# Weights decoded in the tile that they are read into, most reciprocals of two batches taken by way of DRAM, and new ranks, in a pooled-attention kernel with two feed-forward layers

## The chip, the cores and the metric

The kernel runs on one core of one Trainium2 chip. The metric is the device time in microseconds of one execution. The core has TensorE (PE in the rows, its weight loads PEld), VectorE (DVE), ScalarE (ACT), GpSimd (POOL) and SyncE (SP), which here issues most DMAs. TensorE has two levels of clock, 1.2 and 2.4 GHz; the profile gives the granted share.

## The reference

Four batches of eight heads; q, k and v have 1152 rows of 64. Pairs of rows of q are averaged, so 576 queries stand against 1152 keys; softmax with 1e-9 added to the sum; then two feed-forward layers over the 2304 rows of 512.

```python
q_pool = q.reshape(B, H, S // 2, 2, D).mean(axis=3)
scores = 1 / sqrt(D) * q_pool @ k.T
attn = exp(scores - max(scores))
x = attn / (attn.sum(-1) + 1e-9) @ v       # to (4 * 576, 512)
y = (s * relu(x @ w_in) ** 2 + b) @ w_out  # 512 -> 2048 -> 512
out = (sigmoid(y @ w_gate) * (y @ w_val)) @ w_out2   # 512 -> 1536 -> 512
```

The five weights come in as 64-bit floats. The kernel reads each as pairs of 32-bit words.

## The kernel before

Every large operand is split into a rounded high part and the rest, both in a format that TensorE multiplies at its full rate, and each product is made of three matmuls (lines 523 to 525 and 1000 to 1002) or, in the attention, of two or three.

*Attention.* The heads go in pairs. The first batch is done by rows of queries (`pair_rows`); the other three by columns (`pair_half`): each pair in two halves of 288 queries, each half for its two heads in turn. For one head `scores` makes nine blocks of 128 keys by 288 queries (line 752), ACT copies each to SBUF and DVE keeps a running maximum in a tile `mx`; the maximum goes over partitions by transposes (765, 730), is subtracted (DVE) and the exponent taken (ACT, 778). `half_head_sums` rounds the result to a high and a low part (`pp` tiles) and multiplies by v beside columns of ones (800, 801, 805), so that 64 rows of the bank hold x and the other 64 hold the same sum of the softmax, 64 times. ACT writes the sums of both heads, plus 1e-9, to one tile of 128x288 (810), DVE takes its reciprocal (822), and DVE or POOL multiplies x by it (823). In the second and third batch (`DIRECT`) x lies in a tile of SBUF that the feed-forward then splits (`load_split`); in the fourth, each half is stored to DRAM.

*Decode.* `decode` turns one 128x512 block of weights into high and low parts: a load of the pairs of words (`raw`, two tiles), a clamp of the upper words ("w top", 481, DVE or POOL, into a tile `dg`), a scaling ("w scale", ACT), a shift of the lower words ("w low", 485, DVE, into a tile `du`), two operations that join them ("w join" 488, "w sign" 491, DVE), a rounding ("w hi", ACT or POOL) and the rest ("w lo", DVE or POOL). There is one `dg` and one `du`. The first layer's 32 blocks are decoded for the first batch and kept in DRAM; later batches fetch them by POOL's queue (505). The second layer's 36 blocks are decoded twice, once for two batches each.

*Order.* Nothing is issued directly. All operations are added to a `Plan` with an engine or two, an assumed duration, the tiles they need from a number of rooms (`ROOM`) and a rank; `Plan.order` plays the whole program through with these durations and writes out one fixed order for each engine, SP's DMAs included. An engine takes the ready operation of the lowest rank. `MOVED` shifts the rank and the place in a tie of every kind of operation by a table written out by hand. On the chip each engine then works through its list strictly in order and waits by semaphores. So the feed-forward of one batch fills gaps of the attention of the next, as the table lets it.

Of the kernel before, what the change touches and what calls it, by code (L numbers as in the profile page):

```python
# [11 lines left out]
F32 = mybir.dt.float32  # L12
F32R = mybir.dt.float32r
AF = mybir.ActivationFunctionType
# [8 lines left out]


ROOM = dict(
    w=4, raw=2, dg=1, du=1, xy=2, xx=1, r=2, g=4,
    qn=1, kn=1, vn=1, qT=2, kT=2, vt=2, st=6, pp=6,
    sg=2, mx=3, mc=2, r3=2, ts=1, r9=2, x=1, o=2, s=2,
    yy=2, yl=1, h=4, fo=9,
    ps=4, pr=8, pm=1, acc=5, ff=6, p2=3, bank=8,  # L30
)
# [4 lines left out]


MOVED = {
    "q load": (-40, -122),
    "k load": (-5, -76),  # L40
    "v load": (44, 80),
    "v hi": (-12.5, -104),
    "v lo": (0, 12),
    "q add": (-28.5, 49),
    "q twice": (22, -83),
    "pr qT": (0, 83),
    "pr q hi False": (4.5, 33),
    "pr q lo False": (8, 30),
    "pr q hi True": (0, -76),
    "pr q lo True": (10, -85),  # L50
    "pr kT": (0, 17),
    "pr k hi": (-38.5, 40),
    "pr k lo": (-13, 67),
    "s b load": (0, -46),
    "r qk 1": (0, 238),
    "r max": (30, 219),
    "r - max": (-32, 31),
    "r exp": (21.5, -10),
    "r pT": (-18.5, -7),
    "r p": (-8, 9),  # L60
    "r p hi": (-2.5, -73),
    "r p lo": (-24.5, 146),
    "r pv": (-21, 58),
    "r pT hi": (-7, 104),
    "r pT lo": (44, 48),
    "r o": (-27.5, -23),
    "r x add": (52, -90),
    "r qk 2": (-1, -9),
    "r sums": (-8, -48),
    "r sums eps": (-24, -76),  # L70
    "r 1 / sums": (-9, -19),
    "r spread": (-22, -73),
    "r rows": (-1.5, -88),
    "r rows mid": (0, 341),
    "r x / sums": (0, -15),
    "r x / sums mid": (39, 38),
    "r end": (9.5, 29),
    "ps qT": (0, -24),
    "ps q hi False": (25.5, -60),
    "ps q lo False": (6, 36),  # L80
    "ps kT": (-0.5, -14),
    "ps k hi": (0, -132),
    "ps k lo": (-7, -33),
    "xx hi": (0, 74),
    "xx lo": (-12, -44),
    "w load": (-30, -37),
    "w top": (0, -2),
    "w scale": (-5.5, -17),
    "w low": (-13, -15),
    "w join": (-25.5, -49),  # L90
    "w sign": (-16, 89),
    "w hi": (-40, 12),
    "w lo": (-33.5, -64),
    "w keep": (-21, -47),
    "ff xx up": (46.5, -84),
    "ff relu": (0, 11),
    "square": (-30.5, -41),
    "g hi": (-1, -52),
    "g lo": (-32.5, -66),
    "ff down": (24, -66),  # L100
    "column sums": (58.5, -82),
    "column sum": (42, 14),
    "ff y": (-0.5, 39),
    "ff y add": (7.5, -20),
    "bias": (23, -78),
    "y bias": (19.5, -63),
    "y store": (-40, -99),
    "qk": (-3, -4),
    "s copy": (0, 41),
    "s max": (-0.5, 5),  # L110
    "max T": (0, -4),
    "max": (46.5, 5),
    "max rows": (13, -116),
    "s - max": (9.5, -46),
    "exp": (12.5, 16),
    "p hi": (-33.5, -85),
    "p lo": (51.5, -18),
    "pv hi": (13.5, -11),
    "pv lo": (20.5, 90),
    "sums": (14, 71),  # L120
    "x": (42.5, -28),
    "1 / sums": (60, 83),
    "x / sums": (11.5, -116),
    "w fetch": (42.5, -51),
    "w come": (-31, 87),
    "x store": (0, -158),
    "turn": (0, -29),
    "yy load": (-3, 83),
    "yy hi": (16, -21),
    "yy lo": (3, 111),  # L130
    "p2 yy up": (60, 26),
    "gate": (-30, 45),
    "gate val": (-5, 35),
    "h hi": (30, -36),
    "h lo": (28, 88),
    "down 2": (-36, 27),
    "out": (-11, 22),
    "out add": (5.5, 54),
    "out store": (-24, 145),
    "xx load": (59, -89),  # L140
    "p2 xx up": (-1.5, 27),
    "p2 relu": (0, 42),
    "p2 down": (0, -67),
    "p2 y": (-11.5, -107),
    "p2 y add": (0, 78),
}


# [193 lines left out]
def kernel(  # L342
# [124 lines left out]


    def decode(src, w, gate, rank):
        raw = slot("dec", "raw", [P, 512, 2], U32)  # L470
        g = slot("dec", "dg", [P, 512], F32)
        u = slot("dec", "du", [P, 512], U32)

        def fetch():
            if len(src.shape) == 3:
                nc.sync.dma_start(out=raw.t.rearrange("p (k f) t -> p k (f t)", f=P), in_=src)
            else:
                nc.sync.dma_start(out=raw.t.rearrange("p f t -> p (f t)"), in_=src)

        dma("w load", P * 4096, fetch, gate, [raw], rank)  # L480
        shared("w top", 512, lambda e: ENGINE[e].tensor_scalar(
            out=g.t, in0=raw.t[:, :, 1].bitcast(F32), scalar1=F64_TOP, scalar2=-F64_TOP, op0=ALU.min, op1=ALU.max,
        ), [raw], [g], rank, 3.66, fast=True)
        act("w scale", 512, lambda: nc.scalar.mul(g.t, g.t, 2.0 ** -112), [], [g], rank)
        dve("w low", 512, lambda: nc.vector.tensor_scalar(
            out=u.t, in0=raw.t[:, :, 0], scalar1=29, scalar2=None, op0=ALU.logical_shift_right,
        ), [raw], [u], rank, True)
        dve("w join", 512, lambda: nc.vector.scalar_tensor_tensor(
            out=u.t, in0=g.t.bitcast(U32), scalar=3, in1=u.t, op0=ALU.logical_shift_left, op1=ALU.bitwise_or,
        ), [g], [u], rank, port=True)  # L490
        dve("w sign", 512, lambda: nc.vector.scalar_tensor_tensor(  # L491
            out=u.t, in0=g.t.bitcast(U32), scalar=0x80000000, in1=u.t, op0=ALU.bitwise_and, op1=ALU.bitwise_or,
        ), [g], [u], rank, port=True)
        copy_sb("w hi", 512, lambda: w.t[:, 0, :], lambda: u.t.bitcast(F32), [u], [(w, 0)], rank)
        tt_sb("w lo", 512, lambda: w.t[:, 1, :], lambda: u.t.bitcast(F32), lambda: w.t[:, 0, :].bitcast(F32), ALU.subtract,
              [u, (w, 0)], [(w, 1)], rank)

    def weights(pair, gate=(), rank=FE, keep=False, kept=False):

# [290 lines left out]
    def half_head_sums(hf, j, qT, kT, vt, x, sums):  # L790
# [19 lines left out]
        act("sums", HQ + 112, lambda: nc.scalar.activation(  # L810
            out=sums.t[js], in_=acc.t[D:, :HQ], func=AF.Identity, bias=eps[D:, 0:1], scale=1.0), [acc], [(sums, j)], SK, sbuf=False)
        xt, xk = x
        copy_ps("x", HQ, lambda: xt()[js], lambda: acc.t[:D, :HQ], [acc], [(*xk, j)], SK)

    def pair_half(b, hp, hf, prep):
        qT, kT, vt = prep
        x = slot("sm", "x", [P, HQ]) if b not in DIRECT else xs[b]
        xt, xk = ((lambda: x.t[:, hp, hf * HQ:(hf + 1) * HQ]), (x, hp, hf)) if b in DIRECT else ((lambda: x.t), (x,))
        sums = slot("sm", "s", [P, HQ])
        for j in range(2):  # L820
            half_head_sums(hf, j, qT[j], kT[j], vt[j], (xt, xk), sums)
        dve("1 / sums", HQ * 6, lambda: nc.vector.reciprocal(out=sums.t, in_=sums.t), [], [(sums, 0), (sums, 1)], SK)
        tt_sb("x / sums", HQ, xt, xt, lambda: sums.t, ALU.mult,
              [(sums, 0), (sums, 1)], [(*xk, 0), (*xk, 1), *([(x, hp, hf)] if b in DIRECT else [])], SK)
# [6 lines left out]
    def pair_rows(hp, prep, x):  # L831
# [52 lines left out]
        def group(j, g, blocks, mid):  # L884
# [4 lines left out]
            for c0 in range(0, NK, step):  # L889
# [209 lines left out]
```

## Time and profile before

| | us |
|---|---|
| three runs | 1484.94, 1485.54, 1489.52 |
| median | 1485.54 |
| profiled execution | 1490.57 |
| its span, first to last instruction | 1488.8 |
| PE busy in the span | 1411.6 (95%) |
| DVE, ACT, POOL busy | 1111.9 (75%), 946.2 (64%), 667.6 (45%) |
| mean granted clock of TensorE | 0.981 |

The profiled execution is a fourth execution, with 5.0 us more than the median. Busy shares are over the whole span. The attention fills about the first 890 us; the last 600 are feed-forward alone.

### The profile page before, as it was taken

How to read it: one execution, taken by the hardware profiler on the slowest of the kernel's cores; microseconds unless marked ns; L12 is line 12 of the kernel's file. 1: busy time of each engine (PE TensorE's matmuls, PEld its weight loads, DVE VectorE, ACT ScalarE, POOL GpSimd, SP SyncE). 2: the span in 40 equal slices, each digit the busy share in tenths (PEclk: the TensorE clock that was granted, in tenths of full speed). 3: DMA queues.
4: the chain of work that ended last, by engine and by line, in shares of the span. 5: the costliest groups of instructions: out<-in, count | busy, mean ns of one | idle time of the engine just before them, and what ended most of it. 6: DMA issues, size and time to landing. Idle time of an engine off the chain costs nothing.

```text
span 1488.8 us, 26268 instructions
## 1 busy us (share of the span) xinstructions
PE 1411.6 (95%) x9868; PEld 1346.4 (90%) x9868; DVE 1111.9 (75%) x1848; ACT 946.2 (64%) x2030; POOL 667.6 (45%) x555
## 2 busy tenths in 40 slices
PE   7998899897979999999999999999999999999998
PEld 6887789897869999999999999989998999989897
DVE  6899898889998988888998867667674125757562
ACT  6889888868777989779889965434241524434140
POOL 3666465646575666547766635312222002313120
PEclk9999999899989999999999999999999999999999
DMA  3234313342532513323250335433234543333122
GB/s 88 77 117 155 105 57 106 122 145 94 179 112 82 177 35 144 125 68 103 74 190 24 130 141 204 163 99 99 72 100 121 184 170 100 100 96 103 58 71 64
DMA packets 98510, 165.79 MB, mean 111 GB/s; under 512 B 41936, under 2 KB 75728, under 8 KB 89296
## 3 DMA queue, kind: packets, MB, share of 16 engines
q1 hardware_dynamic: 91472, 113.79, 24.8%
q0 software_dynamic: 6912, 50.33, 9.5%
q8 instruction: 77, 1.26, 0.3%
q14 instruction: 49, 0.40, 0.1%
HBM read 137.89 MB, written 26.21 MB: 110 GB/s over the span
## 4 chain that ended last, share of the span: by engine, by line
PE 73%; DVE 11%; ACT 10%; issue 4%; POOL 1%; DMA 0%; DVEq 0%; ACTq 0%; POOLq 0%
PE banks L523 14%; PE banks L525 14%; PE banks L524 14%; PE banks L752 5%; PE banks L1000 3%; PE banks L1001 3%; PE banks L1002 3%; PE banks L800 3%; PE banks L801 3%; DVE mx L463 3%; PE banks L805 3%; PE banks L920 2%; ACT st L457 2%; PE banks L853 2%; ACT kT L457 2%
## 5 line engine op out<-in xcount | busy, mean ns | idle before, releaser
L525 PE MATMUL banks<-yy,w 128*128 128x288 f32 x768 | 226.4, 295 | 0.0
L524 PE MATMUL banks<-yy,w 128*128 128x288 f32 x768 | 226.2, 294 | 0.0
L523 PE MATMUL banks<-yy,w 128*128 128x288 f32 x768 | 226.0, 294 | 0.0
L460 POOL TENSOR_TENSOR pp<-st,pp 128x864 fp32r<-128x864 f32 x96 | 203.7, 2131 | 36.6 <-ACT pp L450 25.0
L457 ACT COPY st<-banks 128x288 f32<-128x288 f32 x432 | 154.0, 412 | 42.7 <-PE banks L752 31.0
L463 DVE TENSOR_TENSOR mx<-banks,mx 128x288 f32<-128x288 f32 x336 | 151.1, 451 | 27.3 <-ACT st L457 15.1
L752 PE MATMUL banks<-qT,kT 128*128 128x288 f32 x864 | 162.0, 308 | 6.0 <-DVE mx L463 3.8
L523 PE MATMUL banks<-xx,w 128*128 128x288 f32 x512 | 154.5, 302 | 1.6 <-ACT r L593 1.2
L524 PE MATMUL banks<-xx,w 128*128 128x288 f32 x512 | 151.1, 295 | 0.6 <-POOL xx L460 0.6
L525 PE MATMUL banks<-xx,w 128*128 128x288 f32 x512 | 151.0, 295 | 0.0
L463 DVE TENSOR_TENSOR st<-st,banks 128x864 f32<-128x864 f32 x144 | 146.5, 1042 | 5.0 <-PE banks L730 5.0
L778 ACT ACTIVATE st<-st 128x864 f32<-128x864 f32 x144 | 133.4, 936 | 24.2 <-DVE st L463 23.2
L450 ACT CAST w<-du 128x512 fp32r<-128x512 f32 x100 | 62.2, 622 | 132.6 <-DVE du L491 91.2
L523 PEld LDWEIGHTS banks<-yy,w 128*128 128x128 f32 x768 | 144.1, 188 | 0.3
L524 PEld LDWEIGHTS banks<-yy,w 128*128 128x128 f32 x768 | 144.0, 188 | 0.3
L525 PEld LDWEIGHTS banks<-yy,w 128*128 128x128 f32 x768 | 144.0, 188 | 0.0
L752 PEld LDWEIGHTS banks<-qT,kT 128*128 128x128 f32 x864 | 132.1, 195 | 11.3 <-DVE mx L463 6.6
L523 PE MATMUL banks<-g,w 128*128 128x288 f32 x448 | 138.6, 309 | 2.0 <-DVE mx L463 1.4
L800 PE MATMUL banks<-pp,vt 128*128 128x288 f32 x432 | 124.7, 308 | 10.6 <-ACT pp L450 7.5
L525 PE MATMUL banks<-g,w 128*128 128x288 f32 x448 | 133.1, 297 | 0.0
L524 PE MATMUL banks<-g,w 128*128 128x288 f32 x448 | 133.0, 297 | 0.0
L801 PE MATMUL banks<-pp,vt 128*64 128x288 f32 x432 | 121.4, 301 | 0.0
(147 smaller groups left out, 3895.6 us busy)
## 6 DMA issues: line engine op xcount, KB each, us to landing
w<-d_1u_1u POOLq DMA_DIRECT2D x24, 1024.0 KB, 6.1
w<-d_1d_1d POOLq DMA_DIRECT2D x24, 1024.0 KB, 6.2
raw<-in_moe_w_out_dram SPq DMA_DIRECT2D x40, 512.0 KB, 3.4
raw<-in_moe_w_gate_dram SPq DMA_DIRECT2D x24, 512.0 KB, 3.6
raw<-in_moe_w_val_dram SPq DMA_DIRECT2D x24, 512.0 KB, 3.5
qn<-in_q_dram SPq DMA_DIRECT2D x16, 576.0 KB, 4.5
kn<-in_k_dram SPq DMA_DIRECT2D x32, 288.0 KB, 4.1
vn<-in_v_dram SPq DMA_DIRECT2D x32, 288.0 KB, 2.8
```

Of the source, the lines that this page charges most:

```text
L450: nc.scalar.copy(out=out(), in_=in_())
L457: act(name, n, lambda: nc.scalar.copy(out=out(), in_=in_()), r, w, rank, sbuf=False)
L460: shared(name, n, lambda e: ENGINE[e].tensor_tensor(out=out(), in0=in0(), in1=in1(), op=op), r, w, rank, 2.15)
L463: dve(name, n, lambda: nc.vector.tensor_tensor(out=out(), in0=in0(), in1=in1(), op=op), r, w, rank)
L523: nc.tensor.matmul(ps(), lhsT=whi(), rhs=xhi(), start=first, stop=False)
L524: nc.tensor.matmul(ps(), lhsT=whi(), rhs=xlo(), start=False, stop=False)
L525: nc.tensor.matmul(ps(), lhsT=wlo(), rhs=xhi(), start=False, stop=last)
L752: nc.tensor.matmul(ps.t[:, :HQ], lhsT=kT.t[:, c], rhs=qq[:, w, hf * HQ:(hf + 1) * HQ], start=(w == 0), stop=(w == 1))
L778: act("exp", 3 * HQ, lambda s=s: nc.scalar.activation(out=s.t, in_=s.t, func=AF.Exp), [], parts, AT)
L800: nc.tensor.matmul(acc.t[:, :HQ], lhsT=vt.t[:, 3 * i + c, D:], rhs=hi.t[:, c], start=(i == c == 0), stop=False)
L801: nc.tensor.matmul(acc.t[:D, :HQ], lhsT=vt.t[:, 3 * i + c, :D], rhs=hi.t[:, c], start=False, stop=False)
L805: nc.tensor.matmul(acc.t[:, :HQ], lhsT=vt.t[:, 3 * i + c, D:], rhs=lo.t[:, c], start=False, stop=(i == c == 2))
```

## The change

Four groups of things are changed.

- `decode` keeps everything in `raw`: the upper words are clamped and scaled where they lie, the lower words shifted, joined and signed where they lie. Its operations thus read and write every second word. `dg` and `du` are gone; there are three `raw` tiles for two. The duration that the plan assumes for "w top" on POOL goes from 105 + 3.66 ns an element to 105 + 1.08.
- In the second and third batch, for all halves but each batch's last, the sums of the two heads (now written as one row each) go to DRAM as 2 x 288 numbers, come back as 64 rows of nine, are inverted there, go to DRAM again and come back spread over 64 rows for each head. The last half of each batch, and the whole fourth batch, keep the reciprocal of 128x288.
- Rooms: `mx` two tiles for three, `r9` one for two, new tiles `rs` and `rr`, one each; the first batch's output copy ("r o") takes a `pp` tile instead of one of its own.
- Each new operation has a rank of its own, and the table `MOVED` is written anew for all others too.

```diff
-    w=4, raw=2, dg=1, du=1, xy=2, xx=1, r=2, g=4,
+    w=4, raw=3, xy=2, xx=1, r=2, g=4,
...
-    sg=2, mx=3, mc=2, r3=2, ts=1, r9=2, x=1, o=2, s=2,
+    sg=2, mx=2, mc=2, r9=1, x=1, s=2, rs=1, rr=1,
...
-    "q load": (-40, -122),
+    "q load": (8, -97),
...
-    "w fetch": (42.5, -51),
-    "w come": (-31, 87),
+    "w fetch": (-8, 31),
+    "w come": (0, -52),
...
         raw = slot("dec", "raw", [P, 512, 2], U32)
-        g = slot("dec", "dg", [P, 512], F32)
-        u = slot("dec", "du", [P, 512], U32)
+        low, top = (raw, 0), (raw, 1)
+
+        def words(i):
+            return raw.t[:, :, i]
...
         shared("w top", 512, lambda e: ENGINE[e].tensor_scalar(
-            out=g.t, in0=raw.t[:, :, 1].bitcast(F32), scalar1=F64_TOP, scalar2=-F64_TOP, op0=ALU.min, op1=ALU.max,
-        ), [raw], [g], rank, 3.66, fast=True)
+            out=words(1).bitcast(F32), in0=words(1).bitcast(F32), scalar1=F64_TOP, scalar2=-F64_TOP, op0=ALU.min, op1=ALU.max,
+        ), [], [top], rank, 1.08, fast=True)
...
         dve("w low", 512, lambda: nc.vector.tensor_scalar(
-            out=u.t, in0=raw.t[:, :, 0], scalar1=29, scalar2=None, op0=ALU.logical_shift_right,
-        ), [raw], [u], rank, True)
+            out=words(0), in0=words(0), scalar1=29, scalar2=None, op0=ALU.logical_shift_right,
+        ), [], [low], rank, True)
         dve("w join", 512, lambda: nc.vector.scalar_tensor_tensor(
-            out=u.t, in0=g.t.bitcast(U32), scalar=3, in1=u.t, op0=ALU.logical_shift_left, op1=ALU.bitwise_or,
-        ), [g], [u], rank, port=True)
+            out=words(0), in0=words(1), scalar=3, in1=words(0), op0=ALU.logical_shift_left, op1=ALU.bitwise_or,
+        ), [top], [low], rank, port=True)
...
+    def inverse(sums, both):
+
+        uid[0] += 1
+        s_d, r_d = (dram.tile([2, HQ], F32, name=f"{n}_{uid[0]}") for n in ("s_d", "r_d"))
+        rs = slot("sm", "rs", [64, 2 * HQ // 64])
+        rr = slot("sm", "rr", [P, HQ])
...
+        dma("sums out", 2304, lambda: nc.sync.dma_start(out=s_d, in_=sums.t.rearrange("(j p) q -> j p q", j=2)[:, 0]),
+            both, [(rs, "out")], SK)
+        dma("sums in", 2304, lambda: nc.sync.dma_start(out=rs.t, in_=spread(s_d)), [(rs, "out")], [rs], SK)
+        dve("1 / sums spread", 54, lambda: nc.vector.reciprocal(out=rs.t, in_=rs.t), [], [rs], SK)
+        dma("1 / sums out", 2304, lambda: nc.sync.dma_start(out=spread(r_d), in_=rs.t), [rs], [(rr, "out")], SK)
+
+        def back():
+            for j in range(2):
+                nc.sync.dma_start(out=rr.t[j * D:(j + 1) * D], in_=r_d[j:j + 1, :].to_broadcast([D, HQ]))
+
+        dma("1 / sums in", P * HQ * 4, back, [(rr, "out")], [rr], SK)
+        return rr, [rr]
...
+        last = b == B - 1 or hp == NP - 1 and hf == 1
...
-        dve("1 / sums", HQ * 6, lambda: nc.vector.reciprocal(out=sums.t, in_=sums.t), [], [(sums, 0), (sums, 1)], SK)
+        if last:
+            dve("1 / sums", HQ * 6, lambda: nc.vector.reciprocal(out=sums.t, in_=sums.t), [], both, SK)
+            inv = sums
+        else:
+            inv, both = inverse(sums, both)
...
-            o = slot("sm", "o", [P, 320])
+            o = slot("pp", "pp", [P, 3 * HQ])
```

## Rows read from the trace of the kernel before

**Rows 1.** The page, busy tenths in 40 slices of 37.2 us, and clock.
```profile
PE   7998899897979999999999999999999999999998
...
PEclk9999999899989999999999999999999999999999
```

**Rows 2.** Stretches: start:end, length, busy us of engines (instructions), clock, DMA share, GB/s.
```profile
75.00:190.00 115.00, 99.14 (x668) 90.22 (x667) 102.67 (x216) 101.25 (x285) 66.27 (x71) 0.94 0.39 122
190.00:447.00 257.00, 225.08 (x1568) 215.48 (x1568) 230.20 (x357) 201.06 (x406) 155.38 (x111) 0.92 0.36 119
447.00:890.00 443.00, 432.15 (x3223) 417.37 (x3222) 384.60 (x617) 371.02 (x765) 269.17 (x199) 1.00 0.33 105
890.00:1489.00 599.00, 592.88 (x4009) 566.82 (x4008) 336.85 (x531) 215.66 (x406) 137.53 (x121) 1.00 0.35 114
```

**Rows 3.** PE's waits (total us, times, longest): two of 190:447, two of 447:890.
```profile
PE banks L800 <- ACT pp L450: 7.5, 1, 7.5
PE banks L765 <- DVE mx L463: 5.0, 2, 4.0
...
PE banks L730 <- DVE mc L769: 3.6, 6, 0.9
...
PE banks L765 <- DVE kT L463: 0.5, 2, 0.3
```

**Rows 4.** Tile s: duration ns min/median/max; and the 128x9 reciprocal (busy us, mean ns).
```profile
L810 ACT ACTIVATE s<-banks,eps x48: 496/498/502, 221.4 to 876.6; 64x288 f32<-64x288 f32 x48
L822 DVE RECIPROCAL s<-s x24: 1934/1942/1954, 227.3 to 877.1; 128x288 f32<-128x288 f32 x24
...
L943 DVE RECIPROCAL r<-r 128x9 f32<-128x9 f32 x4 | 0.8, 203 | 0.0
```

**Rows 5.** The reciprocals of line 822 alone, by stretch: DVE busy us (count).
```profile
190.00:452.00 262.00, 13.62 (x7) 0.92 0.37 121
...
495.00:700.00 205.00, 13.59 (x7) 1.00 0.36 116
700.00:890.00 190.00, 17.48 (x9) 1.00 0.31 103
```

**Rows 6.** Small DMAs: store of x (start ns, landing us), then loads of 512 bytes.
```profile
L827 SPq DMA_DIRECT2D x_d<-x x8: 319/326/332, 729.7 to 880.2; - x8
...
DMA to landing us min/median/max: 1.7/1.7/7.7
...
DMA to landing us min/median/max: 3.6/4.2/4.9
```

**Rows 7.** Decode steps over the span, ns min/median/max; the zeroing of qm (mean).
```profile
L481 POOL TENSOR_SCALAR dg<-raw x52: 635/654/1324, 70.9 to 1434.5; 128x512 f32<-128x512 f32 x52
L485 DVE TENSOR_SCALAR du<-raw x104: 362/427/2322, 74.1 to 1442.5; 128x512 uint32<-128x512 uint32 x104
L488 DVE SCALAR_TENSOR_TENSOR du<-dg,du x104: 673/692/3122, 75.1 to 1442.9; 128x512 uint32<-128x512 uint32 x104
...
L394 DVE CAST qm<-zero 128x512 fp32r<-128x512 f32 x1 | 0.4, 426 | 1.1 <-POOL eps L396 1.1
```

**Rows 8.** Waits of POOL and ACT in 190:447; the last over the span.
```profile
POOL dg L481 <- DVE du L491: 24.7, 8, 6.4
...
ACT w L450 <- DVE du L491: 10.1, 5, 3.3
...
POOL qn L460 <- DMA qn<-in_q_dram: 11.8, 4, 9.0
```

**Rows 9.** SP's own waits in 190:660, the first and the last of fifteen.
```profile
SPq L665 <- POOL vt L460: 98.7, 11, 19.8
...
SPq L478 <- DVE qT L709: 2.2, 2, 1.9
```

**Rows 10.** Join and low in 190:447: count, busy us, mean ns, idle before.
```profile
L488 DVE SCALAR_TENSOR_TENSOR du<-dg,du 128x512 uint32<-128x512 uint32 x23 | 25.2, 1098 | 0.1
L485 DVE TENSOR_SCALAR du<-raw 128x512 uint32<-128x512 uint32 x23 | 19.6, 850 | 0.9 <-POOL w L460 0.8
```

More of the change, by code (lines that the diff above doesn't have):

```diff
@@ L38 @@
 MOVED = {
-    "q load": (-40, -122),
[L40 to L123, printed above, removed]
-    "w fetch": (42.5, -51),
-    "w come": (-31, 87),
[L126 to L145, printed above, removed]
+    "q load": (8, -97),
+    "k load": (16, 21),
+    "v load": (58, -139),
+    "v hi": (-33.5, 17),
+    "v lo": (-5, -53),
+    "q add": (56.5, -16),
+    "q twice": (60, -3),
+    "pr qT": (0, -105),
@@ new lines @@
+    "pr q hi False": (1.5, -26),
+    "pr q lo False": (10, 70),
+    "pr q hi True": (40, 70),
+    "pr q lo True": (4, -76),
+    "pr kT": (-7, 0),
+    "pr k hi": (-23.5, 64),
+    "pr k lo": (4.5, 94),
+    "s b load": (51, 101),
+    "r qk 1": (0, 436),
+    "r max": (20, 94),
+    "r - max": (-33.5, 116),
+    "r exp": (59.5, -13),
+    "r pT": (-31, -29),
+    "r p": (-29.5, -47),
+    "r p hi": (-7.5, -76),
+    "r p lo": (-26.5, 53),
+    "r pv": (-40, 67),
+    "r pT hi": (-20, 30),
+    "r pT lo": (32.5, 157),
@@ new lines @@
+    "r o": (-40, 104),
+    "r x add": (27, -30),
+    "r qk 2": (-29, -108),
+    "r sums": (1.5, -33),
+    "r sums eps": (-0.5, -100),
+    "r 1 / sums": (30, -110),
+    "r spread": (-40, -92),
+    "r rows": (-3, 63),
+    "r rows mid": (0, 533),
+    "r x / sums": (0.5, 3),
+    "r x / sums mid": (52, 49),
+    "r end": (-1, -100),
+    "ps qT": (-6.5, -120),
+    "ps q hi False": (60, 55),
+    "ps q lo False": (-21, 2),
+    "ps kT": (-16, 90),
+    "ps k hi": (2, 116),
+    "ps k lo": (-33.5, 42),
@@ new lines @@
+    "xx hi": (8, 64),
+    "xx lo": (0, -25),
+    "w load": (-40, -77),
+    "w top": (-14.5, 44),
+    "w scale": (-24.5, -15),
+    "w low": (-21, -21),
+    "w join": (0, 65),
+    "w sign": (-30, -67),
+    "w hi": (-33, -111),
+    "w lo": (-40, 113),
+    "w keep": (-34.5, 128),
+    "ff xx up": (42.5, -17),
+    "ff relu": (0, -85),
+    "square": (0.5, 119),
+    "g hi": (0.5, 88),
+    "g lo": (-2, 74),
+    "ff down": (31, 10),
+    "column sums": (60, -1),
+    "column sum": (37.5, 56),
@@ new lines @@
+    "ff y": (-28.5, 61),
+    "ff y add": (19, 52),
+    "bias": (0, -21),
+    "y bias": (0, -25),
+    "y store": (0, -54),
+    "qk": (3.5, -109),
+    "s copy": (4, -73),
+    "s max": (7.5, 39),
+    "max T": (0.5, 25),
+    "max": (60, 105),
+    "max rows": (26.5, 9),
+    "s - max": (22, -81),
+    "exp": (0, 89),
+    "p hi": (-29.5, 0),
+    "p lo": (54.5, -68),
+    "pv hi": (22, 11),
+    "pv lo": (31, 60),
+    "sums": (26, -2),
+    "x": (38, -115),
+    "sums out": (-35, 44),
+    "sums in": (-9.5, 84),
@@ new lines @@
+    "1 / sums spread": (0, -60),
+    "1 / sums out": (-12, -13),
+    "1 / sums in": (22.5, -70),
+    "x / sums": (17, 25),
+    "1 / sums": (24.5, -96),
+    "w fetch": (-8, 31),
+    "w come": (0, -52),
+    "x store": (-3, -88),
+    "turn": (-9, -110),
+    "yy load": (16.5, -72),
+    "yy hi": (13.5, 59),
+    "yy lo": (0, -93),
+    "p2 yy up": (57.5, 61),
+    "gate": (-40, 69),
+    "gate val": (-25.5, 123),
+    "h hi": (0, -7),
+    "h lo": (59.5, 88),
+    "down 2": (-7, 35),
+    "out": (-23, -57),
@@ L146 @@
+    "out add": (11, -115),
+    "out store": (0, -50),
+    "xx load": (-40, 35),
+    "p2 xx up": (-1.5, 75),
+    "p2 relu": (0, -42),
+    "p2 down": (0, 97),
+    "p2 y": (0, -29),
+    "p2 y add": (8, 19),
 }
@@ L478, in fetch @@
                 nc.sync.dma_start(out=raw.t.rearrange("p f t -> p (f t)"), in_=src)
-        dma("w load", P * 4096, fetch, gate, [raw], rank)
+        dma("w load", P * 4096, fetch, gate, [low, top], rank)
         shared("w top", 512, lambda e: ENGINE[e].tensor_scalar(
-            out=g.t, in0=raw.t[:, :, 1].bitcast(F32), scalar1=F64_TOP, scalar2=-F64_TOP, op0=ALU.min, op1=ALU.max,
-        ), [raw], [g], rank, 3.66, fast=True)
-        act("w scale", 512, lambda: nc.scalar.mul(g.t, g.t, 2.0 ** -112), [], [g], rank)
+            out=words(1).bitcast(F32), in0=words(1).bitcast(F32), scalar1=F64_TOP, scalar2=-F64_TOP, op0=ALU.min, op1=ALU.max,
+        ), [], [top], rank, 1.08, fast=True)
@@ L485, in decode @@
+        act("w scale", 512, lambda: nc.scalar.mul(words(1).bitcast(F32), words(1).bitcast(F32), 2.0 ** -112), [], [top], rank)
         dve("w low", 512, lambda: nc.vector.tensor_scalar(
-            out=u.t, in0=raw.t[:, :, 0], scalar1=29, scalar2=None, op0=ALU.logical_shift_right,
-        ), [raw], [u], rank, True)
+            out=words(0), in0=words(0), scalar1=29, scalar2=None, op0=ALU.logical_shift_right,
+        ), [], [low], rank, True)
         dve("w join", 512, lambda: nc.vector.scalar_tensor_tensor(
-            out=u.t, in0=g.t.bitcast(U32), scalar=3, in1=u.t, op0=ALU.logical_shift_left, op1=ALU.bitwise_or,
-        ), [g], [u], rank, port=True)
+            out=words(0), in0=words(1), scalar=3, in1=words(0), op0=ALU.logical_shift_left, op1=ALU.bitwise_or,
+        ), [top], [low], rank, port=True)
@@ L491, in decode @@
         dve("w sign", 512, lambda: nc.vector.scalar_tensor_tensor(
[L492 to L496, printed above, removed]
+            out=words(0), in0=words(1), scalar=0x80000000, in1=words(0), op0=ALU.bitwise_and, op1=ALU.bitwise_or,
+        ), [top], [low], rank, port=True)
@@ L498, in weights @@
+        copy_sb("w hi", 512, lambda: w.t[:, 0, :], lambda: words(0).bitcast(F32), [low], [(w, 0)], rank)
+        tt_sb("w lo", 512, lambda: w.t[:, 1, :], lambda: words(0).bitcast(F32), lambda: w.t[:, 0, :].bitcast(F32), ALU.subtract,
+              [low, (w, 0)], [(w, 1)], rank)
     def weights(pair, gate=(), rank=FE, keep=False, kept=False):
@@ L788, in split_p, with half_head_sums @@
         return hi, lo
-    def half_head_sums(hf, j, qT, kT, vt, x, sums):
+    def half_head_sums(hf, j, qT, kT, vt, x, sums, rows):
         st = scores(hf, qT, kT)
@@ L810, in half_head_sums, with spread @@
         act("sums", HQ + 112, lambda: nc.scalar.activation(
-            out=sums.t[js], in_=acc.t[D:, :HQ], func=AF.Identity, bias=eps[D:, 0:1], scale=1.0), [acc], [(sums, j)], SK, sbuf=False)
+            out=sums.t[j * D:j * D + rows], in_=acc.t[D:D + rows, :HQ], func=AF.Identity, bias=eps[D:D + rows, 0:1], scale=1.0),
+            [acc], [(sums, j)], SK, sbuf=False)
         xt, xk = x
         copy_ps("x", HQ, lambda: xt()[js], lambda: acc.t[:D, :HQ], [acc], [(*xk, j)], SK)
+    def inverse(sums, both):
[3 more added lines that the diff above has]
+        rr = slot("sm", "rr", [P, HQ])
+        def spread(t):
+            return t.rearrange("j (p r) -> (j p) r", r=2 * HQ // 64)
+        dma("sums out", 2304, lambda: nc.sync.dma_start(out=s_d, in_=sums.t.rearrange("(j p) q -> j p q", j=2)[:, 0]),
[8 more added lines that the diff above has]
+        return rr, [rr]
     def pair_half(b, hp, hf, prep):
@@ L819, in pair_half @@
         sums = slot("sm", "s", [P, HQ])
+        last = b == B - 1 or hp == NP - 1 and hf == 1
         for j in range(2):
-            half_head_sums(hf, j, qT[j], kT[j], vt[j], (xt, xk), sums)
-        dve("1 / sums", HQ * 6, lambda: nc.vector.reciprocal(out=sums.t, in_=sums.t), [], [(sums, 0), (sums, 1)], SK)
-        tt_sb("x / sums", HQ, xt, xt, lambda: sums.t, ALU.mult,
-              [(sums, 0), (sums, 1)], [(*xk, 0), (*xk, 1), *([(x, hp, hf)] if b in DIRECT else [])], SK)
+            half_head_sums(hf, j, qT[j], kT[j], vt[j], (xt, xk), sums, D if last else 1)
+        both = [(sums, 0), (sums, 1)]
+        if last:
[3 more added lines that the diff above has]
+            inv, both = inverse(sums, both)
+        tt_sb("x / sums", HQ, xt, xt, lambda: inv.t, ALU.mult,
+              both, [(*xk, 0), (*xk, 1), *([(x, hp, hf)] if b in DIRECT else [])], SK)
         if b in DIRECT:
```

## The prediction

> **What bounds the kernel now.** I read the slices of the span first, then the busy times of the engines in five stretches cut where the slices change, then who keeps TensorE waiting in each stretch, and last the operations that the change touches.
>
> The slices show two kernels in one [rows 1]. From about slice 24 on PE shows 9 in every slice at full clock; before that it falls to 7 in places and the granted clock to 8. The stretches say it in numbers [rows 2]. In 890 to 1489 PE is busy 592.9 of 599 us: nothing that the other engines save there can be had. In 447 to 890 it is idle 443 - 432.2 = 10.8 us. In 190 to 447 it is idle 257 - 225.1 = 31.9 us and its clock is 0.92 on the mean, while DVE is busy 230.2 of 257 us (90%), ACT 78%, POOL 60%. So DVE is the nearest thing to a bound there, and the change's own operations lie there: the second batch's attention, the first batch's first feed-forward and the decode of its weights. In 75 to 190 DVE is at 89% and ACT at 88%, and PE is idle 15.9 us.
>
> The waits of PE agree: in 190 to 447 the largest single one ends on ACT, the next and most of the others on DVE, with the running maxima first [rows 3]. DVE is busy nine tenths of that stretch, so that it is late comes from its amount of work and from its order.
>
> **Reciprocals.** One of 128x288 takes 1.94 us; the 24 of them spread little, 1.934 to 1.954 [rows 4]. One of 128x9 takes 0.203 us [rows 4]; the new one has 64 rows of nine, and I take that price. Each replaced one gives DVE 1.943 - 0.203 = 1.74 us. Seven of eight are replaced in the second batch and seven of eight in the third, 14 x 1.74 = 24.4 us. By place [rows 5]: seven stand in 190 to 452 (second batch), the one in 452 to 495 is that batch's last and stays, the seven of 495 to 700 are the third batch's that go, and of the nine after 700 one is the third batch's last and eight the fourth's, which all stay.
>
> First seven: 7 x 1.74 = 12.2 us out of an engine that is busy 90% of the stretch. I count 0.9 of it, 11 us; the ends are 0 (the rest of the stretch is bound by the order) and 12.2 plus the 2.3 us that DVE waited for ACT's sums in front of two of them, 14.5. Second seven: again 12.2 us, but PE is idle 10.8 us in all of 447 to 890, and the waits that PE has there on DVE are six, from 3.6 down to 0.5 and 7.7 us together, the first and the last of them in [rows 3]. DVE loses 12.2 of 384.6 us of work, a thirtieth; I count 1 us, between 0 and 5.
>
> **The way by DRAM.** Per replaced reciprocal SP issues five DMAs: sums out, sums in, result out, and two broadcasts in. At 0.33 us a start [rows 6] that is 14 x 5 x 0.33 = 23 us of SP. The trip has four landings in a row. The nearest rows: the store of x, 144 KB, lands after 1.7 us at best, a load of 512 bytes to 128 rows after 3.6 and 4.9 [rows 6]. So a trip is 4 x 1.7 = 6.8 to 4 x 4.9 = 19.6 us, and I take 8. It ends in x / sums, whose target in these batches is the x tile that stays in SBUF; the next reader is the split at the batch's end, and the last half, the only one with no time to spare, keeps the old way. In 190 to 452 seven halves come, 37 us each. I count the trip at nothing: the following half hides it. If that cover is gone, one landing of 1.7 us per trip, 24 us over 14, is the price (the slower rival below). The sums instruction on ACT writes one row in place of 64, with the same 288 columns; I take its 0.498 us [rows 4] for the new one too, and if it fell to nothing ACT, at 78%, would gain 28 x 0.5 = 14 us beside the bound.
>
> **Decode in the tile.** All seven steps now walk over every second word; before, only the reads of top and low did. New to it are the writes of top and low, join and sign on DVE, scale on ACT, hi on ACT or POOL, lo on DVE or POOL. For one-input reads the trace shows the price: low reads every second word and takes 0.362 at best, 0.427 in the middle, where a 128x512 cast that walks no second words (the zeroing of qm) takes 0.426 [rows 7]. So reading is free there. No row shows such a write, or a two-input operation with such reads. Ends: nothing, or for 32 decodes up to 447 the loss of low's and top's rate (to join's 0.692, +0.27 each) and twice the time for join and its twin, sign (+0.69 each), 32 x (0.54 + 1.38) = 61 us of DVE. I take nothing, from the nearest row. The Trainium skill says in SBUF — State Buffer, section Door 1: The DMA port swizzle, that words in one 16-byte line come at full bandwidth with two or more hits per line; a step of 8 bytes has two. By that rule the sum would be the same and the strided rival falls away; the trace agrees for reads with the 0.427 us, and no row shows the writes.
>
> What the tile change removes is the two single buffers dg and du. POOL stands 24.7 us in 190 to 447 before w top, until the sign step of the decode before has let go of dg [rows 8], and w top is in order with POOL's lows of p, g and v. With three raw tiles that wait has no cause within three decodes. POOL is at 60% in that stretch and so no bound; ACT's casts lose 10.1 us to the same chain [rows 8]. I count 1 us, between 0 and 12. What is late next is the load: raw was free for its next load after low, and now only after lo. SP waits anyway, fifteen kinds of wait from 98.7 down to 2.2 us and 426 of the 470 us from 190 to 660 together [rows 9]; three tiles against two make up for the longer hold.
>
> The order now books w top on POOL at 105 + 1.08 x 512 = 658 ns in place of 105 + 3.66 x 512 = 1979; the chip takes 654 [rows 7]. The old order thus reserved 1.3 us of POOL too much at each of its 52, 69 us. That is in favour of the new order, but it moves no row by itself: nothing.
>
> **The other ranks and rooms.** Every rank is new, so the order of all engines is new. What an accident of order is worth is shown by the longest wait of PE there, 7.5 us on one rounding of p by ACT [rows 3]. I take nothing as the middle, and one such wait, 7 us, either way. Two mx tiles for three: nothing, as a half needs one and the next half one; a stall for the third would cost PE what its longest wait for a maximum costs, 4.0 us [rows 3]. The output copies of the first batch in pp tiles, one r9 tile: nothing.
>
> **Sum.** -11 - 1 - 1 = -13 us. The profiled execution took 1490.57 us (1488.8 of span and 1.8 around it), so 1477.6 in its terms. The runs are 1484.94, 1485.54 and 1489.52, and their median lies 5.0 under the profiled one: 1472.5, which I forecast as 1473. A measurement of this kernel tells 0.3% (4.5 us) from no change: faster is under 1481.1, slower over 1490.0.
>
> **Rivals.**
> *The port takes the place of the reciprocal (no change).* Join takes 0.692 in the middle but 1.098 on the mean of 190 to 447, and up to 3.1; low 0.850 there for 0.427 [rows 7, 10]. They run long when POOL is at work; the reciprocals never do [rows 4]. So the 12.2 us may be the time in which POOL ran free, and POOL's operations now fall beside joins and signs. The excess there is 23 x (0.41 + 0.42) = 19 us for the two; half as much again would eat 10 of the 13 us: 1482 to 1488. [...] Against the rival: w top's move and the smaller decode chain also change which of the two comes first.
>
> *More than the reciprocals (faster still).* If the dg wait of POOL is what makes the roundings late, on one of which PE stood 7.5 us, and with steadier matmuls the clock returns from 0.92 to 1.00 in part (257 x 0.08 = 20 us at stake), it is 20 to 28 us: 1457 to 1465. For it: the 24.7 us of POOL; against it: PE's waits end mostly on DVE.
>
> *SP held by the trips (slower).* SP works in order. Three of the trip's DMAs wait for a landing or for the reciprocal, so a trip holds SP 3 x 1.7 = 5 us or more, and behind them stand the loads of q, k, v and of raw. SP already stands 90% of 190 to 660, so loads go out when a buffer is free, not earlier; a load held 2 us longer is 2 us late. PE pays only when a preparation has no slack. The point is 13 / 14 = 0.9 us of PE time per trip; past 1.3 us it is slower, and at one landing and a bit, 2 us, the time is 1473 + 28 = 1501. For it: POOL waited for loads of q, 9.0 us at the longest [rows 8]; against it: that is 11.8 us in the whole span.
>
> *Strided steps cost, or the new order is worse.* At a quarter of the upper end, 15 us, 1488; at half, 1503.
>
> **How the numbers follow.** Forecast, 1465 to 1481: 0.47. More: 0.15. Port: 0.19, of which 0.03 is under 1481. SP: 0.12. Strided or order: 0.07. So faster 0.47 + 0.15 + 0.03 = 0.65, same 0.16, slower 0.19. The range 1457 to 1492 leaves out about 0.06 below and 0.13 above.
>
> **What would show it.** Right: ten 128x288 reciprocals and fourteen of 64x9 near 0.2 us; PE idle in the stretch that answers to 190 to 447 down by about 10 us, DVE still near 90%; low, join, sign at 0.43, 0.69, 0.69 in the middle; no wait of POOL at w top on the sign step. Wrong: join and sign means far over 1.1 us (port), waits of POOL or PE that end on loads of q, k or v (SP), low near 0.7 (stride), or a stretch before 190 or after 890 that moves by more than 5 us, which nothing here but the order would do.

## The result, and the profile after

The changed kernel takes 1466.47 us in the median of four runs, the kernel before 1487.37 beside it: ratio 0.9873, interval 0.9825 to 0.992, that is 19 us less (12 to 26). Forecast were 1473 us and 12.5 less. The profiled execution has a span of 1464.1 us.

PE carries out the same 9868 matmuls. In the two profiled executions its idle time falls from 1488.8 - 1411.6 = 77.2 to 1464.1 - 1402.4 = 61.7 us, 15.5 us, and its busy time by 9.2 us, while the mean clock rises from 0.981 to 0.991. Together these are 24.7 us, more than the 19 of the ratio: the profiled execution before was slower than its median (1490.57 against 1487.37), the one after was not (1465.83 against 1466.47). Where the idle time goes, is seen on the page and in the stretches. Here are the slices of the kernel after, which answer to [rows 1]:

```profile
PE   7988999999889999999999999999999999999998
...
PEclk9999999999999999999999999999999999999999
```

No slice of the clock is under nine tenths any more. The stretches of the kernel after, for [rows 2] (us, then busy us of PE, weight loads, DVE, ACT, POOL with instructions; clock, DMA share, GB/s):

```profile
75.00:190.00 115.00, 102.63 (x702) 91.98 (x701) 101.57 (x218) 102.04 (x287) 79.34 (x86) 0.96 0.38 118
190.00:447.00 257.00, 238.60 (x1729) 226.93 (x1730) 224.81 (x386) 217.80 (x443) 185.17 (x127) 0.98 0.41 133
447.00:890.00 443.00, 431.86 (x3215) 417.39 (x3214) 369.92 (x599) 369.10 (x757) 264.32 (x190) 1.00 0.37 121
890.00:1464.00 574.00, 568.22 (x3823) 541.96 (x3821) 323.94 (x447) 196.99 (x360) 210.68 (x186) 1.00 0.33 104
```

In 190 to 447 PE's idle time falls from 31.9 to 18.4 us, its clock rises from 0.92 to 0.98, and it does 1729 matmuls where it did 1568. That is 13.5 of the 15.5 us of idle time; another 3.5 go in 75 to 190, and 1.2 come back before 75. In 447 to 890 nothing moves (10.8 to 11.1). Note who carries the additional work: DVE is no busier (230.2 to 224.8), ACT is busier by 17 and POOL by 30 us.

The wait of 7.5 us on ACT's rounding is gone from the list of PE in 190 to 447 ([rows 3]); none there is over 3 us in total:

```profile
PE banks L813 <- POOL pp L465: 2.9, 5, 1.2
PE banks L531 <- DVE mx L468: 2.9, 2, 2.4
PE banks L760 <- DVE mx L468: 2.4, 3, 1.5
PE banks L808 <- ACT pp L455: 1.6, 2, 1.1
```

The reciprocals, for [rows 4], by lines (busy us, mean ns): as foreseen, ten long ones, and fourteen at 0.2 us.

```profile
L857 DVE RECIPROCAL s<-s 128x288 f32<-128x288 f32 x10 | 19.5, 1946 | 1.7 <-ACT s L818 1.7
...
L837 DVE RECIPROCAL rs<-rs 64x9 f32<-64x9 f32 x14 | 2.8, 201 | 1.1 <-DMA rs<-s_d 1.0
```

The steps of the decode in the kernel after, for [rows 7] (ns at least, in the middle and at most; 493 low, 492 scale, 496 join, 499 sign, 489 top):

```profile
L493 DVE TENSOR_SCALAR raw<-raw x104: 415/432/3582, 73.8 to 1407.2; 128x512 uint32<-128x512 uint32 x104
L492 ACT ACTIVATE raw<-raw x104: 664/687/743, 74.4 to 1408.0; 128x512 f32<-128x512 f32 x104
L496 DVE SCALAR_TENSOR_TENSOR raw<-raw x104: 674/693/2249, 75.2 to 1409.8; 128x512 uint32<-128x512 uint32 x104
L499 DVE SCALAR_TENSOR_TENSOR raw<-raw x104: 675/694/2506, 79.5 to 1411.4; 128x512 uint32<-128x512 uint32 x104
L489 POOL TENSOR_SCALAR raw<-raw x102: 637/844/1163, 73.3 to 1406.8; 128x512 f32<-128x512 f32 x102
```

Join takes 0.693 for 0.692, low 0.432 for 0.427: in the middle, DVE's steps over every second word take what the dense ones took, for writes and for two inputs as well. Scale on ACT takes 0.687 for 0.630, and the last step, w lo on DVE, 1.020 for 0.693; both before, then w lo after:

```profile
L484 ACT ACTIVATE dg<-dg x104: 614/630/726, 73.5 to 1439.8; 128x512 f32<-128x512 f32 x104
```
```profile
L460 DVE TENSOR_TENSOR w<-du,w x57: 674/693/1626, 126.8 to 1445.5; 128x512 fp32r<-128x512 f32 x57
```
```profile
L465 DVE TENSOR_TENSOR w<-raw,w x40: 676/1020/2181, 107.5 to 1414.1; 128x512 fp32r<-128x512 f32 x40
```

Counted by start and end times in the trace, six of these forty overlap no operation of POOL and take 0.676 to 0.693 us; 34 overlap one, and take 1.14 in the middle. Before, 26 of 57 did, and took 0.693 even so. So the step alone shows no cost, and the longer times come beside POOL. The order now gives 102 of 104 tops to POOL (52 before). Join, sign and low in 190 to 447, against [rows 10], which has no row of sign; sign before, then all three after:

```profile
L491 DVE SCALAR_TENSOR_TENSOR du<-dg,du 128x512 uint32<-128x512 uint32 x23 | 22.4, 975 | 0.0
```
```profile
L496 DVE SCALAR_TENSOR_TENSOR raw<-raw 128x512 uint32<-128x512 uint32 x21 | 22.7, 1098 | 0.0
L499 DVE SCALAR_TENSOR_TENSOR raw<-raw 128x512 uint32<-128x512 uint32 x21 | 22.0, 1060 | 0.0
L493 DVE TENSOR_SCALAR raw<-raw 128x512 uint32<-128x512 uint32 x21 | 16.0, 779 | 1.0 <-DMA raw<-in_moe_w_out_dram 0.6 <-DMA raw<-in_moe_w_in_dram 0.4
```

Join's mean is 1.098 us, the same as before; sign is longer and low shorter, and the three together take 2.94 us a block for 2.92; with what DVE has of w top and w lo it is 3.37 for 3.31. So the port did not take the reciprocals' place in this stretch. And for [rows 8] the waits of ACT for the decode and of POOL for w top's data in 190 to 447:

```profile
ACT w L455 <- DVE raw L499: 1.3, 2, 0.8
```
```profile
POOL raw L489 <- DMA raw<-in_moe_w_in_dram: 4.1, 2, 2.6
POOL raw L489 <- DMA raw<-in_moe_w_out_dram: 3.8, 3, 1.7
```

The 24.7 us that POOL stood before w top on the sign step are gone; what is late next is the load, 7.9 us, as the prediction said.

So every sign that the prediction asked for is there. Whether its reasons are right is another matter.

### The profile page after: what moved, and what is told of

The parts are those of the page before. It is cut to its first block, busy times and chain, and to the rows that moved or that the text cites. A ratio compares the mean times of both kernels' runs of the same rounds, so it can differ in the third digit from the quotient of the medians.

```text
span 1464.1 us, 26453 instructions
## 1 busy us (share of the span) xinstructions
PE 1402.4 (96%) x9868; PEld 1334.4 (91%) x9868; DVE 1075.5 (73%) x1775; ACT 944.4 (65%) x2017; POOL 777.3 (53%) x641
## 5 line engine op out<-in xcount | busy, mean ns | idle before, releaser
L465 POOL TENSOR_TENSOR pp<-st,pp 128x864 fp32r<-128x864 f32 x106 | 226.5, 2144 | 47.5 <-ACT pp L455 41.2
L489 POOL TENSOR_SCALAR raw<-raw 128x512 f32<-128x512 f32 x102 | 84.2, 826 | 106.1 <-DMA raw<-in_moe_w_gate_dram 43.3
L760 PEld LDWEIGHTS banks<-qT,kT 128*128 128x128 f32 x864 | 127.7, 188 | 11.1 <-DVE mx L468 5.6
L531 PE MATMUL banks<-g,w 128*128 128x288 f32 x448 | 135.5, 302 | 0.9 <-DVE mx L468 0.8
L533 PE MATMUL banks<-g,w 128*128 128x288 f32 x448 | 132.0, 295 | 0.0
L532 PE MATMUL banks<-g,w 128*128 128x288 f32 x448 | 132.0, 295 | 0.0
L492 ACT ACTIVATE raw<-raw 128x512 f32<-128x512 f32 x104 | 71.6, 688 | 75.7 <-POOL raw L489 73.6
```

Of the source, the lines that this page charges most:

```text
L465: shared(name, n, lambda e: ENGINE[e].tensor_tensor(out=out(), in0=in0(), in1=in1(), op=op), r, w, rank, 2.15)
L489: shared("w top", 512, lambda e: ENGINE[e].tensor_scalar(out=words(1).bitcast(F32), in0=words(1).bitcast(F32), scalar1=F64_TOP, scalar2=-F ...
L492: act("w scale", 512, lambda: nc.scalar.mul(words(1).bitcast(F32), words(1).bitcast(F32), 2.0 ** -112), [], [top], rank)
L531: nc.tensor.matmul(ps(), lhsT=whi(), rhs=xhi(), start=first, stop=False)
L532: nc.tensor.matmul(ps(), lhsT=whi(), rhs=xlo(), start=False, stop=False)
L533: nc.tensor.matmul(ps(), lhsT=wlo(), rhs=xhi(), start=False, stop=last)
```

## The experiments

Three theories: R, the gain is DVE's time for the reciprocals (the prediction's main term); D, it is the decode without the two single buffers; O, it is the order, that is, new ranks and a plan that assumes w top's true price. The ratios below are all against the kernel before, run beside; times "under before" are the ratio's distance from 1 times 1487 us. The kernel after stands at 0.9873.

**The order held, one cost changed.** In these three the plan gets the same numbers as the kernel that it starts from, and so every engine the same list.

Fourteen reciprocals cut short in the kernel before (x is then multiplied by sums that are mostly not inverted):

```diff
+        last = b == B - 1 or hp == NP - 1 and hf == 1
+        part = (lambda: sums.t) if last else (lambda: sums.t[:64, :9])
-        dve("1 / sums", HQ * 6, lambda: nc.vector.reciprocal(out=sums.t, in_=sums.t), ...
+        dve("1 / sums", HQ * 6, lambda: nc.vector.reciprocal(out=part(), in_=part()), ...
```

> The kernel before in its own order, with fourteen reciprocals (all halves of the second and third batch but each batch's last) cut to 64x9, so that x is left unscaled there; no trip, no other change. Theory R (the gain is DVE's time for the reciprocals): 9 to 14 us faster than before, 1473 to 1478. Theory O (the gain is the order: new ranks and a truer plan): under 5 us, 1482 to 1487. Theory D (the gain is the decode without dg and du): under 5 us too.

Measured: 0.9983 (0.9968 to 0.9997), 2.5 us under before, between 0.4 and 4.8. Its reciprocals and its stretch 190 to 447:

```profile
L824 DVE RECIPROCAL s<-s 64x9 f32<-64x9 f32 x14 | 2.8, 198 | 0.0
```
```profile
190.00:447.00 257.00, 223.61 (x1575) 213.80 (x1575) 220.85 (x356) 201.92 (x407) 154.32 (x110) 0.93 0.37 122
```

DVE's busy time falls by 9 us there (from 230.2), and PE does 1575 matmuls for 1568: what DVE no longer does, it now waits. Two of its waits there, 0.5 and 0.8 us before:

```profile
DVE kT L463 <- ACT kT L457: 4.8, 4, 3.3
DVE du L485 <- POOL w L460: 3.8, 4, 1.2
```

R's number is refused.

Fourteen long reciprocals added to the kernel after, on a scratch tile:

```diff
+        def spread_inverse():
+            nc.vector.reciprocal(out=rs.t, in_=rs.t)
+            nc.vector.reciprocal(out=scratch, in_=scratch)
-        dve("1 / sums spread", 54, lambda: nc.vector.reciprocal(out=rs.t, in_=rs.t), [], [rs], SK)
+        dve("1 / sums spread", 54, spread_inverse, [], [rs], SK)
```

> The kernel after in its own order, with one more reciprocal of 128x288 on a scratch tile behind each of the fourteen small ones, 14 x 1.95 us of DVE given back. Theory R: 9 to 14 us slower than after, 1476 to 1480, nearly all of it before 650 us. Theories O and D: under 5 us slower, 1466 to 1471.

Measured: 1.0054 (1.0034 to 1.0075), so (1.0054 - 0.9873) x 1487 = 27 us over after, with some 8 us of error by the two intervals, for this much work of DVE:

```profile
L841 DVE RECIPROCAL scratch<-scratch 128x288 f32<-128x288 f32 x14 | 26.4, 1887 | 0.0
```
```profile
190.00:447.00 257.00, 232.68 (x1638) 221.01 (x1637) 224.93 (x359) 208.17 (x423) 175.81 (x122) 0.95 0.40 129
447.00:890.00 443.00, 423.40 (x3122) 407.23 (x3120) 382.41 (x623) 371.08 (x762) 264.74 (x188) 0.99 0.34 111
```

The time grows by about what was added, in the third batch too, where PE's idle time rises from 11.1 to 19.6 us; no theory expected that. It is not all waiting: between the two profiles PE's idle time grows by 17 us in the span and its busy time by 14, as the mean clock falls from 0.991 to 0.983. Beside the first experiment it says: in these fixed orders, time taken off DVE was hardly found again, and time put on it was paid. That the lists wait for each other is the likely reason; no run shows it for the second. Neither number is the worth of a reciprocal in a new order.

The trip's seventy DMAs taken out of the kernel after (x is multiplied by the sums, not inverted, which ACT writes to 64 rows again in those halves):

```diff
-        dma("sums in", 2304, lambda: nc.sync.dma_start(out=rs.t, in_=spread(s_d)), [(rs, "out")], [rs], SK)
+        dma("sums in", 2304, lambda: None, [(rs, "out")], [rs], SK)
...
```

> The kernel after in its own order, without the seventy DMAs of the trip; the sums are not inverted in those fourteen halves. If the trip costs nothing, as predicted: within 3 us of after, 1464 to 1469. If SP is held by it (the slower rival): 5 us or more faster, under 1461.

Measured: 0.9864 (0.9839 to 0.989) against 0.9873 of after: 1 us, within the error, and none of its four times is under 1461. The trip costs nothing that shows, though most of its landings are longer than the 1.7 us I took as the nearest. In the kernel after, sums in, result out and the broadcasts (start in ns at least, in the middle, at most; then landings in us):

```profile
L836 SPq DMA_DIRECT2D rs<-s_d x14: 448/466/1127, 236.8 to 616.1; - x14
...
DMA to landing us min/median/max: 2.9/4.1/5.2
```
```profile
L838 SPq DMA_DIRECT2D r_d<-rs x14: 460/472/1108, 242.4 to 624.1; - x14
...
DMA to landing us min/median/max: 1.7/2.0/6.3
```
```profile
L842 SPq DMA_DIRECT2D rr<-r_d x28: 444/535/1644, 244.1 to 627.0; - x28
...
DMA to landing us min/median/max: 2.5/2.6/8.3
```

**Ranks.** The kernel after under the table of before:

```diff
-    "q load": (8, -97),
+    "q load": (-40, -122),
... all others too, but for the five new operations
```

> The kernel after with the table of ranks of before (the five new operations keep their new ranks), so the plan gives another order. Theory R: 1466 to 1476, the ranks being worth an accident of order (7 us either way). Theory O: 1480 or more. Theory D: as R.

Measured: 1.024 (1.0217 to 1.0262), 36 us slower than before and 55 slower than after, as O expected. This table, at least, is worth something only with the plan that it was made for, so a part of the change can't be judged with the ranks left as they were. The stretch 75 to 190 shows the damage, 568 matmuls for 702:

```profile
75.00:190.00 115.00, 92.54 (x568) 79.72 (x567) 91.78 (x182) 83.27 (x229) 69.61 (x74) 0.91 0.32 105
```

**Each part with ranks of its own.** For the next eight the table was made anew for each plan by random trying, judged by the length that the plan itself reckons; for each partial kernel twice. How much was tried for each table, and for those of before and after, no run shows.

The kernel before, only the table new:

> The kernel before, with nothing but another table of ranks, searched for anew under the plan's own assumptions. Since with the old ranks the kernel after took 1523 us, ranks are worth tens of us and the parts can only be told apart when each has ranks of its own; this is the base for the next three. Theory O (the order): 1475 to 1487. Theories R and D (the gain comes from the reciprocals or from the decode): no more than 4 us from before, 1482 to 1491.

Measured: 0.9993 (0.9984 to 1.0003), 1485.4 us, which lies in both ranges. This one new table gives nothing. Its stretch 190 to 447:

```profile
190.00:447.00 257.00, 229.18 (x1616) 220.46 (x1616) 240.97 (x364) 211.03 (x424) 177.84 (x120) 0.93 0.38 123
```

The true price of w top added:

```diff
-        ), [raw], [g], rank, 3.66, fast=True)
+        ), [raw], [g], rank, 1.08, fast=True)
```

> As the one before it, with the assumed price of w top on POOL as in the change (1.08 for 3.66 ns an element), and its own searched ranks. Theory O: 8 to 15 us under the kernel with only new ranks, with POOL busier than before. Theories R and D: within 4 us of that kernel.

> The kernel before with the true price of w top alone, under a second searched table, from another start. The first table gave 1471.9. If the price is what counts (theory O): 1466 to 1478 again. If 1471.9 was luck of one order: 1480 or more.

Measured: 0.9903 (0.9885 to 0.9922) and 0.9959 (0.9945 to 0.9974): 14 and 6 us under before, with nothing changed but which engine does a shared operation, and when. The first is what O expected. The second, 1482.3 us, lies where the expectation put "luck of one order" (1480 or more), though it is clear of before. The stretch 190 to 447 of the first and of the second:

```profile
190.00:447.00 257.00, 234.51 (x1674) 223.76 (x1673) 234.47 (x373) 220.20 (x449) 199.53 (x135) 0.95 0.37 121
```
```profile
190.00:447.00 257.00, 227.11 (x1650) 216.75 (x1648) 240.76 (x373) 212.82 (x433) 188.37 (x130) 0.96 0.38 123
```

POOL is busy 199.5 and 188.4 us there, for 155.4 before, and PE gets further. That an order which believes POOL free sooner gives it more is not shown by this: the kernel with only new ranks did it in part too (177.8, and 1616 matmuls), without a shorter time, and over the whole span POOL is busy 722 and 675 us, for 668 both before and with only new ranks.

Price and the way by DRAM, decode as before:

```diff
-        dve("1 / sums", HQ * 6, lambda: nc.vector.reciprocal(out=sums.t, in_=sums.t), ...
+            inv, both = inverse(sums, both)
```

> Price and the way by DRAM (two mx tiles), decode as before, its own searched ranks. Theory R: 9 to 14 us under the kernel with the price alone. Theories O and D: within 4 us of it.

> Price and the way by DRAM under a second searched table; the first gave 1486.2. If the shorter reciprocals are worth their 11 us once the order can use them (theory R): under the second table of the price alone by 5 us or more. If the trip is worth nothing (O): within the spread of the tables, 1470 to 1488, with no side.

Measured: 1.0004 (0.9986 to 1.0022) and 0.9896 (0.9879 to 0.9913), 16 us apart. The first lies 14 us over the first table of the price alone, against R, and outside the 4 us of O and D too. The second, 1473.2, lies 9 us under the second table of the price alone, as R asked, and is also inside the spread that O allowed. The first table's stretches show why one stretch is not the whole:

```profile
190.00:447.00 257.00, 235.24 (x1691) 224.60 (x1691) 232.81 (x378) 223.76 (x455) 190.73 (x124) 0.97 0.42 135
447.00:890.00 443.00, 423.29 (x3114) 405.98 (x3114) 364.20 (x592) 352.64 (x726) 247.38 (x186) 0.99 0.34 108
```

PE does 123 matmuls more than before in 190 to 447 and 109 fewer in 447 to 890.

Price and the decode in the tile, all reciprocals long:

```diff
-    w=4, raw=2, dg=1, du=1, xy=2, xx=1, r=2, g=4,
+    w=4, raw=3, xy=2, xx=1, r=2, g=4,
... and decode as in the change
```

> Price and the decode in the tile (three raw, no dg and du), all 24 reciprocals of 128x288 as before, three mx tiles, its own searched ranks. Theory R: 9 us or more slower than after, over 1475. Theory D: 6 to 15 us under the kernel with the price alone, and no slower than after: 1455 to 1468. Theory O: the same, as the freed tiles count for the order.

> Price and the decode in the tile, all reciprocals long, under a second searched table; the first gave 1484.4. Theory R: over 1475 again, since only the reciprocals are missing against the kernel after at 1466. Theory D: 1455 to 1470. If tables scatter by 15 us (O): anywhere from 1466 to 1486.

Measured: 0.9982 (0.9969 to 0.9995) and 0.9911 (0.9896 to 0.9925), 11 us apart. The first, 1484.4, is over 1475 as R asked, and far from D's 1455 to 1468. The second, 1474.4 with every reciprocal long, lies within its error of R's bound of 1475, over D's range and inside O's.

The kernel after, with the prices of four decode steps raised towards what its own trace shows:

```diff
-        ), [], [top], rank, 1.08, fast=True)
+        ), [], [top], rank, 1.45, fast=True)
-        act("w scale", 512, ...
+        act("w scale", 512 + 68, ...
... w hi on ACT 0.92 for 0.833, w lo on POOL 2.46 for 2.15
```

> The kernel after, with the plan's prices of the four steps that the trace of after shows dearer on every second word (w top on POOL 1.45 ns an element for 1.08, w lo on POOL 2.46 for 2.15, w scale and w hi on ACT 50 to 60 ns more), and ranks searched for under these. If a truer plan is what gains time (theory O): 2 to 12 us under after, 1455 to 1464, with less waiting of ACT for w top. If 1466 was a lucky order: 1470 or more.

Measured: 0.9868 (0.9844 to 0.9892), 1468.6 us: no better than after, and between what the two theories asked. ACT waits less for w top, 55.0 us for 73.6 in the span, without a shorter time; in the kernel after, then in this one:

```profile
ACT raw L492 <- POOL raw L489: 73.6, 45, 8.9
```
```profile
ACT raw L492 <- POOL raw L489: 55.0, 42, 5.7
```

Together, in us under before, the two tables of each ("as before" has its own table first; the two of "all" differ in four prices too):

| | first | second | mean |
|---|---|---|---|
| as before | 0 | 1 | 0.5 |
| price | 14 | 6 | 10 |
| price, way by DRAM | -1 | 16 | 7.5 |
| price, decode in the tile | 3 | 13 | 8 |
| all (after; with the dearer prices) | 19 | 20 | 19 |

What follows: with the price true, every pair lies under before in the mean, by 8 to 10 us, in a scatter of 8 to 16 us between two tables of one kernel; with the old price there are two tables only, at 0 and 1. So that the price gains time is likely, and its size is open. Neither the trip nor the decode shows a gain of its own beyond the price: against the price alone both lose under the first tables, and both gain under the second. Both together lie 19 and 20 under, some 9 us more than the price alone in the mean, but the best partial one, 0.9896, is not clear of after by the intervals. Nor is it only these two that are put together there: the rooms that change besides (one `r9` tile, the first batch's output in a `pp` tile) are in no partial kernel. Which parts make the 19 us stays open.

## Why the prediction was right or wrong

The time, the sign and the place were right: 1466.5 in the range, and most of the idle time went in 190 to 447. That the number came out was in good part luck: the term that made 11 of its 13 us is not borne out, and the runs leave room for the gain in terms that it put at nothing.

*First seven reciprocals, 11 us.* This is the step that failed, and it was the main term. It took DVE's nine tenths of the stretch for a bound, of which work can be taken off. All fourteen, cut short in the old order, gave 2.5 us. In that stretch the time came back as waits of DVE for ACT and POOL. The lower end that I kept, 0 because the rest is bound by the order, was the right one in the old order. With new orders the question stays open: DVE's time put back cost 27 us for 26.4, and the kernels with the trip lie once 14 us over and once 9 under those with the price alone.

*Second seven, 1 us.* PE's idle time in 447 to 890 went from 10.8 to 11.1 us, so nothing, inside the range.

*The two single buffers, 1 us.* The wait of 24.7 us is gone as foreseen. What that is worth is open: the kernels with this decode and the price lie 3 and 13 us under before, those with the price alone 14 and 6.

*Price of w top, nothing.* Probably mis-sized: with it alone, two new tables gave 14 and 6 us, and a new table without it 1. The prediction saw that the plan reserved 69 us of POOL too much, and priced it at nothing because it "moves no row by itself". In a kernel whose order is reckoned from assumed durations, a wrong duration can make a worse order. How is not shown: POOL's busy time in 190 to 447, 155 us before, is 185 in the kernel after and 188 to 200 with the price alone, but 178 with new ranks alone.

*Ranks, 7 us either way.* Too small: two tables of one kernel lie up to 16 us apart, and a table of another plan costs 55 us. The longest wait of PE is no measure of that.

*Strided steps, nothing.* Right where it mattered, on DVE: join takes 0.693 for 0.692. The Trainium skill's rule (SBUF — State Buffer, section Door 1: The DMA port swizzle: two hits in a 16-byte line suffice for full bandwidth) agrees with that, for join's write and two inputs as well. ACT departs from it: scale takes 0.687 for 0.630, and the measurement decides.

*The trip, nothing.* Right: 1 us within the error. The three landings shown make 8.7 us in the middle, without the first of the trip, for which no landing is on record; 8 us were taken for all four. The slower rival falls with it: SP does wait for the landings, but taking all of the trip's DMAs away gave no time.

*The port rival.* It falls in its stretch, with join, sign and low at 2.94 us a block for 2.92. It is right elsewhere: after 890 join and sign rise from 0.693 and 0.757 to 0.918 and 1.114 us in the mean, some 35 us of DVE in all, where PE is busy 99% and it costs nothing that shows. Join and sign that overlap no operation of POOL take 0.67 to 0.70 us before and after, and one that does up to 3.1. Low, which has one input, behaves alike: 0.43 us at most by itself in the kernel before, up to 2.3 beside POOL.

*The clock.* "More than the reciprocals" set a rise of the clock beside the gain, and it did rise, from 0.978 to 0.987 in the runs of the kernel before (thirteen, beside the first experiments) to 0.985 to 0.992 in the four of the kernel after. That steadier matmuls raised it, no run shows, and a higher clock is not by itself a shorter time: with the price and the way by DRAM under the first table it is 0.990 and the time that of before, as PE is idle 72 us, for 62 in the kernel after. The fall of 9.2 us in busy time comes partly from the slow profile before: the fourteen reciprocals cut short show 1402.4 us of busy time too, at 2.5 us of gain.

*The chances.* The strided rival is counted as slower, though at a quarter, 1488 us, it is still "same" by the prediction's own bounds.

## What to carry to other kernels

An engine that is busy nine tenths in a stretch is not thereby the bound: shorten its work with the order held, and see whether the others follow, before counting a gain. Where an order is computed from assumed durations, compare these with the trace first; one false price may have cost this kernel as much as fourteen long reciprocals were thought to. And compare parts of such a change only with an order made for each, more than once, since two orders of the same program differ here by 1%.

## What the runs showed of the hardware that was not expected

- On DVE, writing every second word, or reading two operands so, costs nothing: join takes at least 0.674 and in the middle 0.693 us, for 0.673 and 0.692 dense. On ACT it does cost: the scaling in place on every second word is 57 ns longer (0.687 for 0.630, all 104 above the old middle), and the rounding that only reads so is 45 ns longer (0.666 for 0.621).
- w top on POOL has the same floor, 0.637 for 0.635 us, but its middle went from 0.654 to 0.844. It goes with what runs beside it: the 12 of 102 that overlap only those operations of DVE that read a PSUM bank take 0.644 to 0.673 us, and the 46 that overlap only others 0.878 in the middle. Before, 47 of 52 overlapped one that reads a bank. The stride alone shows no cost there.
- DMAs of 2.2 KB in pieces of 36 bytes start in 0.47 us where a store of x starts in 0.33, and land in 2.0 (to DRAM) and 4.1 us (from it).
